# A gated recurrence with an expert layer on one core: wider transposes, evictions by PSUM bank, another order of the same operations

## The chip, the cores and the metric

The kernel runs on one core of a Trainium2 chip. The metric is the device time of one execution in microseconds. Before the change it was 181.66 us (median of 3 runs, 180.91 to 183.07). The engines are TensorE (PE, with its weight loads PEld), VectorE (DVE), ScalarE (ACT), GpSimd (POOL), and SyncE (SP), which gives out most transfers. [...]

## The reference

A recurrence runs over 768 steps for 4 sequences of 8 heads, with a state of 48 x 48 per head that decays by `w`. Its output goes through an expert layer with a maximum of two products.

```python
# r, k, v, w: (4, 8, 768, 48);  u: (8, 48);  w1, w2: (384, 1024);  w_out: (1024, 384)
for t in range(S):
    cur = einsum('bhd,bhe->bhde', u * k[t], v[t])
    y[t] = einsum('bhd,bhde->bhe', r[t], state + cur)
    state = w[t][..., None] * state + einsum('bhd,bhe->bhde', k[t], v[t])
x = y.transpose(0, 2, 1, 3).reshape(3072, 384)
out = maximum(x @ w1, x @ w2) @ w_out
```

## The kernel before

The work is cut into 12 units: 3 chunks of 256 steps for each of 4 sequences. Unit n is chunk n // 4 of sequence n % 4. A partition holds two steps that follow each other (i = 0, 1), and the 128 partitions form two blocks b of 64. The decay within a block is turned into factors on r and k (`rp`, `kp`), so that a block is a masked product of k and r, and the state passes from block to block.

The program is a list of operations, `ORDER`. The body walks through it and records each one; every engine then runs its share in that order. A name is an operation and, after the point, a unit (for weights a third of the rows). What the names do:

- loads on SyncE: `w`, `k`, `r`, `v` (384 KB each), `u`, `w1`; on GpSimd, with a cast to bf16: `w2`, `wo`; `wt` is a transposing load of w2 on SyncE
- weights: `wd` = w1 - w2 (VectorE); `wcm` = w2 x w_out (TensorE), evicted by `wce` (VectorE). With these, max(x w1, x w2) w_out = relu(x wd) w_out + x wc
- factors: `lw` = ln w (ScalarE), `lp` sum of pairs (GpSimd), `cs` running sum over the steps (TensorE, fp32), `m`, `z` (VectorE), `AO`, `AE`, `iA` exponentials (ScalarE), `rp`, `kp` products with r and k (VectorE)
- the term of u: `rk`, `rku` (GpSimd), `dg` (VectorE), `vd` (GpSimd); `vb` is v in bf16 (GpSimd)
- `tr`: transposes of r and k to PSUM; `evr` (ScalarE) and `evk` (VectorE) bring them to SBUF
- state: `kv` (TensorE), `Sa`, `Tf` (VectorE), `S1` (ScalarE), `dec`, `S0` (GpSimd); `row`, `WL` carry the last row of the factors onto partitions, `Wt` is its exponential
- `sc0`, `sc1` products of k and r (TensorE), `M0`, `M1` the masked copies (VectorE), `yb`, `yi`, `ya` the output in PSUM (TensorE), `xT` its copy (ScalarE)
- the expert layer: `g0` to `g3` (TensorE), `r0` to `r3` the relu (ScalarE), `oc`, `oa`, `ob` (TensorE), `os` the copy (ScalarE), `out` the store (SyncE, two transfers)

The parts that the change touches:

```python
@op
def tr(n):
    U[n]["tr"] = tp = pt_([P, 2, 2, 2, NP, Q], BF16, "sc")      # [128, b, j, i, p, 64]: two banks
    for j, src in enumerate((r_b, k_b)):
        for i in range(2):
            for p in range(NP):                                  # NP = 4 pairs of heads
                for e in range(2):
                    for b in range(2):
                        q = slice(b * Q, (b + 1) * Q)
                        nc.tensor.transpose(tp[e * DP:(e + 1) * DP, b, j, i, p, :],
                                            src[n % 2][q, i, 2 * p + e, :], ident[q, q])

def evict(n, j, copy):                                           # j: r or k, out of both banks
    U[n]["rk"[j] + "T"] = t = wt_([P, 2, 2, NP, Q], BF16, "rk"[j] + "T")
    copy(t.rearrange("d b i p q -> d b (i p q)"),
         U[n]["tr"][:, :, j].rearrange("d b i p q -> d b (i p q)"))

OP["evr"] = lambda n: evict(n, 0, nc.scalar.copy)
OP["evk"] = lambda n: evict(n, 1, nc.vector.tensor_copy)
...
def scores(n, i):
    rT, kT = U[n]["rT"], U[n]["kT"]
    U[n]["sc", i] = sc = pt_([P, 2, NP, P], F32, "sc")           # the same PSUM buffer as tr
    ...
                nc.tensor.matmul(sc[q, e, p, :], kT[d, b, i, p, :], rT[d, b, :, p, :])
```

Buffers: the PSUM buffers `sc` (transposes and scores), `y` and `ex` are single, `go` (expert layer) is double; the loads have three buffers each.

Of the kernel before, what the change touches and what calls it, by code (L numbers as in the profile page):

```python
# [23 lines left out]
vd.2 ob0.0 os0.0 oc1.0 oa1.0 ob1.0 os1.0 kp.2 kv.2 tr.2 Sa.2 evr.2 Tf.2 S1.2 cs.3 WL.0 Wt.0
dec.0 S0.0 g0.1 r0.1 evk.2 row.2 WL.2 Wt.2 row.1 m.3 WL.1 AO.3 z.3 AE.3 yb.2 yi.2 sc0.2 M0.2
g1.1 r1.1 g2.1 r2.1 sc1.2 M1.2 g3.1 oc0.1 oa0.1 r3.1 k.3 r.3 rk.3 rku.3 rp.3 v.3 w.4 lw.4 lp.4
vb.3 iA.3 dg.3 vd.3 ya.2 xT.2 ob0.1 os0.1 oc1.1 oa1.1 Wt.1 dec.1 S0.1 kp.3 kv.3 tr.3 Sa.3 Tf.3
evr.3 S1.3 cs.4 m.4 AO.4 z.4 AE.4 evk.3 ob1.1 os1.1 g0.2 r0.2 yb.3 yi.3 sc0.3 M0.3 out0.0 g1.2
g2.2 r1.2 r2.2 row.3 WL.3 Wt.3 sc1.3 M1.3 g3.2 r3.2 oc0.2 oa0.2 k.4 r.4 rk.4 rku.4 rp.4 v.4 w.5
lw.5 lp.5 vb.4 dg.4 vd.4 iA.4 ya.3 xT.3 ob0.2 os0.2 oc1.2 oa1.2 out1.0 kp.4 kv.4 tr.4 Sa.4 evr.4  # L30
Tf.4 S1.4 cs.5 m.5 AO.5 z.5 AE.5 evk.4 ob1.2 os1.2 g0.3 r0.3 row.4 WL.4 out1.1 yb.4 yi.4 sc0.4
M0.4 g1.3 g2.3 r1.3 r2.3 sc1.4 M1.4 g3.3 r3.3 oc0.3 oa0.3 k.5 r.5 rk.5 rku.5 rp.5 v.5 w.6 lw.6
lp.6 vb.5 iA.5 dg.5 vd.5 ya.4 xT.4 ob0.3 os0.3 oc1.3 oa1.3 out0.1 row.5 WL.5 kp.5 kv.5 tr.5 Sa.5
evr.5 Tf.5 S1.5 cs.6 m.6 AO.6 z.6 AE.6 evk.5 ob1.3 os1.3 g0.4 r0.4 yb.5 yi.5 sc0.5 M0.5 g1.4
g2.4 r1.4 r2.4 out1.2 dec.2 Wt.4 Wt.5 S0.2 sc1.5 M1.5 g3.4 r3.4 oc0.4 oa0.4 out0.2 k.6 r.6 rk.6
rku.6 rp.6 v.6 w.7 lw.7 lp.7 vb.6 dg.6 vd.6 iA.6 ya.5 xT.5 out0.3 ob0.4 os0.4 oc1.4 oa1.4 kp.6
kv.6 tr.6 Sa.6 evr.6 Tf.6 S1.6 cs.7 m.7 AO.7 z.7 AE.7 evk.6 dec.3 S0.3 ob1.4 os1.4 g0.5 r0.5
yb.6 yi.6 sc0.6 M0.6 row.6 WL.6 Wt.6 out1.3 g1.5 g2.5 r1.5 r2.5 sc1.6 M1.6 g3.5 r3.5 oc0.5 oa0.5
k.7 r.7 rk.7 rku.7 rp.7 v.7 w.8 lw.8 lp.8 vb.7 iA.7 dg.7 vd.7 ya.6 xT.6 out0.4 ob0.5 os0.5 oc1.5
oa1.5 kp.7 kv.7 tr.7 Sa.7 evr.7 Tf.7 S1.7 cs.8 m.8 AO.8 z.8 AE.8 evk.7 dec.4 S0.4 ob1.5 os1.5  # L40
g0.6 r0.6 yb.7 yi.7 sc0.7 M0.7 g1.6 g2.6 r1.6 r2.6 row.7 WL.7 Wt.7 out1.4 sc1.7 M1.7 g3.6 r3.6
oc0.6 oa0.6 k.8 r.8 rk.8 rku.8 rp.8 v.8 w.9 lw.9 lp.9 vb.8 iA.8 dg.8 vd.8 ya.7 xT.7 out0.5 ob0.6
os0.6 oc1.6 oa1.6 kp.8 kv.8 tr.8 Sa.8 evr.8 S1.8 cs.9 m.9 AO.9 z.9 AE.9 evk.8 ob1.6 os1.6 g0.7
r0.7 yb.8 yi.8 sc0.8 M0.8 dec.5 S0.5 g1.7 g2.7 r1.7 r2.7 out1.5 sc1.8 M1.8 g3.7 r3.7 oc0.7 oa0.7
k.9 r.9 rk.9 rku.9 rp.9 v.9 w.10 lw.10 lp.10 vb.9 iA.9 dg.9 vd.9 ya.8 xT.8 out0.6 ob0.7 os0.7
oc1.7 oa1.7 kp.9 tr.9 kv.9 Sa.9 evr.9 S1.9 cs.10 m.10 AO.10 z.10 AE.10 evk.9 dec.6 S0.6 ob1.7
os1.7 g0.8 r0.8 yb.9 yi.9 sc0.9 M0.9 g1.8 g2.8 r1.8 r2.8 sc1.9 M1.9 g3.8 r3.8 oc0.8 oa0.8 out1.6
k.10 r.10 rk.10 rku.10 rp.10 v.10 w.11 lw.11 lp.11 vb.10 dg.10 vd.10 iA.10 ya.9 xT.9 out0.7
ob0.8 os0.8 oc1.8 oa1.8 kp.10 kv.10 tr.10 Sa.10 evr.10 S1.10 cs.11 m.11 AO.11 z.11 AE.11 evk.10
ob1.8 os1.8 g0.9 r0.9 yb.10 yi.10 sc0.10 M0.10 dec.7 S0.7 g1.9 g2.9 r1.9 r2.9 out1.7 sc1.10  # L50
M1.10 g3.9 r3.9 oc0.9 oa0.9 k.11 r.11 rk.11 rku.11 rp.11 v.11 vb.11 iA.11 dg.11 vd.11 ya.10
xT.10 out0.8 ob0.9 os0.9 oc1.9 oa1.9 kp.11 tr.11 kv.11 Sa.11 evr.11 S1.11 evk.11 ob1.9 os1.9
g0.10 r0.10 yb.11 yi.11 sc0.11 M0.11 g1.10 g2.10 r1.10 r2.10 sc1.11 M1.11 out1.8 out1.9 g3.10
# [24 lines left out]

def _body(tc, r, k, v, w, u_in, moe_w1, moe_w2, moe_w_out, out):
    nc = tc.nc  # L80
    B, H, S, D = r.shape
# [235 lines left out]
    @op  # L317
    def tr(n):
        U[n]["tr"] = tp = pt_([P, 2, 2, 2, NP, Q], BF16, "sc")
        for j, src in enumerate((r_b, k_b)):  # L320
            for i in range(2):
                for p in range(NP):
                    for e in range(2):
                        for b in range(2):
# [1 line left out]
                            nc.tensor.transpose(tp[e * DP:(e + 1) * DP, b, j, i, p, :],  # L326
                                                src[n % 2][q, i, 2 * p + e, :], ident[q, q])

    def evict(n, j, copy):
        U[n]["rk"[j] + "T"] = t = wt_([P, 2, 2, NP, Q], BF16, "rk"[j] + "T")  # L330
        copy(t.rearrange("d b i p q -> d b (i p q)"),  # L331
             U[n]["tr"][:, :, j].rearrange("d b i p q -> d b (i p q)"))
# [49 lines left out]


    def scores(n, i):
        rT, kT = U[n]["rT"], U[n]["kT"]
        U[n]["sc", i] = sc = pt_([P, 2, NP, P], F32, "sc")
        for p in range(NP):
            for b in range(2):
                q = slice(b * Q, (b + 1) * Q)
                for e in range(2):  # L390
                    d = slice(e * DP, e * DP + D)
                    nc.tensor.matmul(sc[q, e, p, :], kT[d, b, i, p, :], rT[d, b, :, p, :])  # L392
# [156 lines left out]
```

## Time and profile before

| | |
|---|---|
| time, median of 3 | 181.66 us (180.91 to 183.07) |
| span of the profiled run (its time 180.87) | 179.0 us |
| mean granted TensorE clock | 0.986 |
| instructions in the profile | 7356 |
| VectorE, ScalarE, GpSimd busy | 99.3, 94.3, 93.7 us |
| moved by the transfers | 28.24 MB, mean 158 GB/s |

A line of a group has the source line, the engine and the operation, then output <- inputs by the program's names, the shapes and the count; after the bar the busy time in us and the mean ns of one; after the second bar the idle time of that engine just before, and what ended it. A line of the timeline has the start and the length in us, then the same names. A line of the waits has who waited for whom, the total in us, how often, and the longest. In the row of 40 slices each digit is the busy share of one slice (4.5 us here) in tenths. "issue" is a wait for nothing that the profile shows. w_sb is w2 in SBUF.

### The profile page before, as it was taken

Reading aid. Unit: us, or ns where it says so; the run is one execution under the profiler, and the core shown is the slowest. Engines: PE = TensorE matmul, PEld = TensorE weight load, DVE = VectorE, ACT = ScalarE, POOL = GpSimd, SP = SyncE. Lnnn points to the kernel's source line nnn. Section 1 sums busy time; section 2 is a strip of 40 time slices with the busy share of each in tenths; the row PEclk is TensorE's granted clock in tenths of the full one; section 3 lists DMA queues with packets and bytes.
Section 4 is the critical chain, followed back from the end, with each engine's and each line's share of the span. In section 5 each row is a group of like instructions: output and inputs, shape, how many; then the busy total and the mean of one; then the engine's idle time right before and its main releaser. Section 6 shows DMA issues by size and latency. Waiting matters only on the chain.

```text
span 179.0 us, 7356 instructions
## 1 busy us (share of the span) xinstructions
PE 137.7 (77%) x3304; PEld 91.1 (51%) x3304; DVE 99.3 (55%) x144; ACT 94.3 (53%) x165; POOL 93.7 (52%) x91
## 2 busy tenths in 40 slices
PE   0323722779968978969989899896897898999990
...
GB/s 154 202 217 304 297 108 143 296 272 85 85 290 31 182 221 44 268 139 74 198 222 163 276 57 277 147 247 178 44 278 125 80 265 14 49 4 92 64 31 87
DMA packets 63184, 28.24 MB, mean 158 GB/s; under 512 B 58152, under 2 KB 62376, under 8 KB 63152
## 3 DMA queue, kind: packets, MB, share of 16 engines
...
q0 software_dynamic: 1440, 1.57, 5.5%
q8 instruction: 26, 0.43, 0.9%
...
HBM read 23.81 MB, written 4.73 MB: 159 GB/s over the span
## 4 chain that ended last, share of the span: by engine, by line
PE 54%; issue 13%; DVE 9%; POOL 6%; ACT 4%; DMA 0%; DVEq 0%; POOLq 0%; ACTq 0%
PE go L493 14%; PE go L469 14%; PE go L488 6%; PE sc L392 5%; PE ex L237 4%; PE sc L326 4%; PE y L453 3%; DVE kT L331 3%; DVE mz L251 3%; DVE mz L247 3%; ACT ex L255 2%; PE y L346 2%; POOL rku L297 2%; PE y L432 1%; POOL rku L302 1%
## 5 line engine op out<-in xcount | busy, mean ns | idle before, releaser
L469 PE MATMUL go<-xT,wd_sb 128*128 128x256 bf16 x288 | 38.2, 277 | 1.8 <-ACT gT L477 1.8
L493 PE MATMUL go<-wo_sb,gT 128*128 128x384 bf16 x192 | 38.5, 327 | 0.0
L477 ACT ACTIVATE gT<-go 128x512 bf16<-128x512 f32 x48 | 28.5, 599 | 15.0 <-PE go L469 14.3
L396 DVE TENSOR_TENSOR M<-sc,mask 128x1024 bf16<-128x1024 f32 x24 | 29.4, 1224 | 12.5 <-PE sc L392 12.4
L469 PEld LDWEIGHTS <-wd_sb 128*128 128x128 bf16 x288 | 26.9, 99 | 9.0 <-issue 2.7
L233 POOL TENSOR_TENSOR lp<-lw 128x384 f32<-128x384 f32 x12 | 12.0, 1000 | 34.0 <-ACT lw L228 34.0
L297 POOL TENSOR_TENSOR rku<-lr,lk 128x768 f32<-128x768 f32 x12 | 21.7, 1810 | 15.3 <-issue 13.2
L493 PEld LDWEIGHTS <-gT 128*128 128x128 bf16 x192 | 17.8, 98 | 13.6 <-issue 1.8
L331 ACT COPY rT<-sc 128x1024 bf16<-128x1024 bf16 x12 | 12.1, 1012 | 20.8 <-PE sc L326 20.8
L302 POOL TENSOR_TENSOR rku<-rku,u_b 128x768 f32<-128x768 f32 x12 | 21.8, 1813 | 1.8 <-DMA u_b<-in_u_dram 1.0
L313 POOL TENSOR_TENSOR vd<-lv,dg 128x768 bf16<-128x768 f32 x12 | 17.7, 1475 | 3.9 <-DVE dg L308 3.9
L237 PE MATMUL ex<-lp,triS 128*128 128x384 f32 x24 | 13.2, 635 | 7.7 <-POOL lp L233 6.1
L228 ACT ACTIVATE lw<-lw 128x768 f32<-128x768 f32 x12 | 10.0, 837 | 13.3 <-DMA lw<-in_w_dram 13.3
L488 PE MATMUL go<-wc_sb,xT 128*128 128x384 bf16 x72 | 15.6, 326 | 0.0
L392 PE MATMUL sc<-rT,kT 48*64 48x128 bf16 x384 | 10.7, 229 | 6.3 <-DVE kT L331 5.2
L247 DVE TENSOR_TENSOR mz<-ex,lw 128x384 f32<-128x384 f32 x12 | 6.7, 557 | 14.4 <-PE ex L237 14.4
L498 ACT COPY osb<-go 128x384 f32<-128x384 f32 x24 | 11.5, 481 | 5.1 <-PE go L493 5.1
L362 DVE TENSOR_TENSOR Sa<-y,Sf 128x256 f32<-128x256 f32 x12 | 5.1, 425 | 15.3 <-PE y L346 15.3
L392 PEld LDWEIGHTS <-kT 48*64 48x64 bf16 x384 | 6.6, 110 | 11.9 <-DVE kT L331 6.8
L308 DVE TENSOR_REDUCE dg<-rku 128x16 f32<-128x768 f32 x12 | 11.4, 947 | 1.8 <-POOL rku L302 1.8
L255 ACT ACTIVATE ex<-mz 128x384 f32<-128x384 f32 x12 | 5.9, 495 | 11.8 <-DVE mz L247 7.2
L267 DVE TENSOR_TENSOR rn<-lr,ex 128x768 bf16<-128x768 f32 x12 | 11.3, 945 | 1.1 <-ACT ex L259 1.1
...
## 6 DMA issues: line engine op xcount, KB each, us to landing
lw<-in_w_dram SPq DMA_DIRECT2D x12, 384.0 KB, 6.0
lk<-in_k_dram SPq DMA_DIRECT2D x12, 384.0 KB, 3.6
lr<-in_r_dram SPq DMA_DIRECT2D x12, 384.0 KB, 4.5
lv<-in_v_dram SPq DMA_DIRECT2D x12, 384.0 KB, 5.5
...
wo_sb<-in_moe_w_out_dram POOLq DMA_DIRECT2D x1, 768.0 KB, 11.1
...
```

Source lines behind the costliest of these rows:

```text
L237: nc.tensor.matmul(EX[:, 0, 0:HD], triS, U[n]["lp"].rearrange("p h d -> p (h d)"))
L247: nc.vector.tensor_add(MZ[n % 2][:, 0, :, 0:D], ex3(), U[n]["lw"][:, :, 0, :])
L297: nc.gpsimd.tensor_mul(t, U[n]["r"], U[n]["k"])
L302: nc.gpsimd.tensor_mul(t, t, u_b.rearrange("p (h d) -> p h d", h=H).unsqueeze(1).to_broadcast([P, 2, H, D]))
L313: nc.gpsimd.tensor_mul(t.rearrange("p i h d -> p h i d"), U[n]["v"], U[n]["dg"].to_broadcast([P, H, 2, D]))
L331: copy(t.rearrange("d b i p q -> d b (i p q)"), U[n]["tr"][:, :, j].rearrange("d b i p q -> d b (i p q)"))
L392: nc.tensor.matmul(sc[q, e, p, :], kT[d, b, i, p, :], rT[d, b, :, p, :])
L396: nc.vector.tensor_mul(t.rearrange("s e p t -> s (e p) t"), U[n]["sc", i].rearrange("s e p t -> s (e p) t"), mask[:, i].rearrange("s i q - ...
L469: nc.tensor.matmul(g[:, f, :], wd_sb[:, ko, fo * P:(fo + 1) * P], U[n]["xT"][:, :, ko, :], start=(f == 0 and ko == 0), stop=(f == 1 and ko ...
L477: nc.scalar.activation(U[n]["gT"][:, 2 * j:2 * j + 2].rearrange("p f j t -> p (f j t)"), U[n]["g", j].rearrange("p f j t -> p (f j t)"), A ...
L488: nc.tensor.matmul(t, U[n]["xT"][:, b, ko, :], wc_sb[:, ko, :], start=(ko == 0), stop=False)
L493: nc.tensor.matmul(U[n]["o", b], U[n]["gT"][:, fo, b, :], wo_sb[:, fo, :], start=False, stop=(fo == FO - 1))
```

## The change

A transpose now takes two heads at once (64 rows, 128 columns), so that a unit has 32 of them and not 64. The PSUM tile has one bank for each block b. The two evictions are cut by block and no longer by r and k, so that each reads a bank of its own; this is for running ScalarE and VectorE at the same time. The readers (`scores` and the product with the state) take r and k from the tile of their block.

```diff
-                    for e in range(2):
-                        for b in range(2):
-                            q = slice(b * Q, (b + 1) * Q)
-                            nc.tensor.transpose(tp[e * DP:(e + 1) * DP, b, j, i, p, :],
-                                                src[n % 2][q, i, 2 * p + e, :], ident[q, q])
+                    for b in range(2):
+                        q = slice(b * Q, (b + 1) * Q)
+                        nc.tensor.transpose(
+                            tp[:, b, j, i, p, :],
+                            src[n % 2][q, i, 2 * p:2 * p + 2, :].rearrange("s e d -> s (e d)"),
+                            ident[q, q])
...
-    def evict(n, j, copy):
-        U[n]["rk"[j] + "T"] = t = wt_([P, 2, 2, NP, Q], BF16, "rk"[j] + "T")
-        copy(t.rearrange("d b i p q -> d b (i p q)"),
-             U[n]["tr"][:, :, j].rearrange("d b i p q -> d b (i p q)"))
+    def evict(n, b, copy):
+        U[n]["T", b] = t = wt_([P, 2, 2, NP, Q], BF16, f"T{b}")
+        copy(t.rearrange("d j i p q -> d (j i p q)"),
+             U[n]["tr"][:, b].rearrange("d j i p q -> d (j i p q)"))
-    OP["evr"] = lambda n: evict(n, 0, nc.scalar.copy)
-    OP["evk"] = lambda n: evict(n, 1, nc.vector.tensor_copy)
+    OP["ev0"] = lambda n: evict(n, 0, nc.scalar.copy)
+    OP["ev1"] = lambda n: evict(n, 1, nc.vector.tensor_copy)
...
-                    nc.tensor.matmul(sc[q, e, p, :], kT[d, b, i, p, :], rT[d, b, :, p, :])
+                    nc.tensor.matmul(sc[q, e, p, :], t[d, 1, i, p, :], t[d, 0, :, p, :])
```

The list `ORDER` is replaced as a whole by one found in another search; the operations are the same. Its beginning, and one steady stage of each (unit 5 in the recurrence, unit 4 in the expert layer):

```diff
 # the beginning
-w.0 k.0 lw.0 r.0 u wo lp.0 cs.0 m.0 z.0 AO.0 AE.0 rp.0 rk.0 rku.0 dg.0 iA.0 kp.0 tr.0 evr.0
-evk.0 v.0 vb.0 kv.0 Sa.0 Tf.0 w.1 lw.1 S1.0 k.1 vd.0 yb.0 yi.0 sc1.0 M1.0 lp.1 cs.1 m.1 AO.1
-sc0.0 M0.0 ya.0 xT.0 z.1 AE.1 w1 w2 wt.1 wcm.1 wd.2 wd.0 wd.1 wce.1 r.1 rk.1 rku.1 rp.1 v.1 vb.1
-w.2 lw.2 lp.2 iA.1 dg.1 vd.1 row.0 g0.0 g1.0 r0.0 r1.0 g2.0 r2.0 kp.1 kv.1 Sa.1 S1.1 tr.1 evr.1
-Tf.1 cs.2 m.2 AO.2 z.2 AE.2 evk.1 wt.0 wcm.0 wce.0 yb.1 yi.1 sc0.1 M0.1 wt.2 ...
+w.0 lw.0 k.0 r.0 u w2 rk.0 rku.0 dg.0 lp.0 cs.0 m.0 z.0 AO.0 AE.0 rp.0 iA.0 kp.0 v.0 vb.0 w.1 w1
+wd.0 k.1 r.1 lw.1 kv.0 Sa.0 Tf.0 S1.0 tr.0 ev0.0 ev1.0 wd.1 wo lp.1 cs.1 m.1 z.1 AO.1 AE.1 vd.0
+yb.0 yi.0 sc0.0 M0.0 sc1.0 rp.1 M1.0 iA.1 kp.1 rk.1 rku.1 dg.1 wd.2 ya.0 xT.0 tr.1 ev0.1 ev1.1
+v.1 vb.1 w.2 wt.0 wt.1 wcm.0 lw.2 wce.0 kv.1 Sa.1 S1.1 Tf.1 wcm.1 wce.1 g0.0 r0.0 vd.1 yb.1 yi.1
+sc0.1 M0.1 g1.0 g2.0 r1.0 r2.0 sc1.1 M1.1 row.0 WL.0 Wt.0 lp.2 cs.2 m.2 z.2 AO.2 AE.2 wt.2 ...
 # a steady stage
-kp.5 kv.5 tr.5 Sa.5 evr.5 Tf.5 S1.5 cs.6 m.6 AO.6 z.6 AE.6 evk.5 ob1.3 os1.3 g0.4 r0.4 yb.5 yi.5
-sc0.5 M0.5 g1.4 g2.4 r1.4 r2.4 out1.2 dec.2 Wt.4 Wt.5 S0.2 sc1.5 M1.5 g3.4 r3.4 oc0.4 oa0.4 out0.2
-k.6 r.6 rk.6 rku.6 rp.6 v.6 w.7 lw.7 lp.7 vb.6 dg.6 vd.6 iA.6 ya.5 xT.5 out0.3 ob0.4 os0.4 oc1.4 oa1.4
+tr.5 ev0.5 ev1.5 ob1.3 os1.3 out1.3 g0.4 r0.4 kv.5 Sa.5 S1.5 Tf.5 lp.6 cs.6 m.6 z.6 g1.4 r1.4 g2.4
+r2.4 vd.5 yb.5 yi.5 sc0.5 M0.5 AO.6 AE.6 rp.6 g3.4 r3.4 oc0.4 oa0.4 sc1.5 M1.5 iA.6 kp.6 rk.6
+rku.6 dg.6 v.6 w.7 lw.7 k.7 r.7 vb.6 ob0.4 oc1.4 oa1.4 os0.4 out0.4 row.5 WL.5 dec.3 S0.3 ya.5 xT.5
...
```

In the new list the loads of w, of w2 and of the next unit stand earlier, and `tr` of a unit stands before the expert layer's work of the unit before it.

More of the change, by code (lines that the diff above doesn't have):

```diff
@@ L17 @@
 ORDER = """
-w.0 k.0 lw.0 r.0 u wo lp.0 cs.0 m.0 z.0 AO.0 AE.0 rp.0 rk.0 rku.0 dg.0 iA.0 kp.0 tr.0 evr.0
-evk.0 v.0 vb.0 kv.0 Sa.0 Tf.0 w.1 lw.1 S1.0 k.1 vd.0 yb.0 yi.0 sc1.0 M1.0 lp.1 cs.1 m.1 AO.1
-sc0.0 M0.0 ya.0 xT.0 z.1 AE.1 w1 w2 wt.1 wcm.1 wd.2 wd.0 wd.1 wce.1 r.1 rk.1 rku.1 rp.1 v.1 vb.1
-w.2 lw.2 lp.2 iA.1 dg.1 vd.1 row.0 g0.0 g1.0 r0.0 r1.0 g2.0 r2.0 kp.1 kv.1 Sa.1 S1.1 tr.1 evr.1
-Tf.1 cs.2 m.2 AO.2 z.2 AE.2 evk.1 wt.0 wcm.0 wce.0 yb.1 yi.1 sc0.1 M0.1 wt.2 wcm.2 wce.2 sc1.1
-M1.1 g3.0 oc0.0 oa0.0 r3.0 k.2 r.2 rk.2 rku.2 rp.2 v.2 w.3 lw.3 lp.3 vb.2 iA.2 ya.1 xT.1 dg.2
@@ L24 @@
[L24 to L53, printed above, removed]
@@ L54 @@
-r3.10 oc0.10 oa0.10 ya.11 xT.11 out0.9 ob0.10 os0.10 oc1.10 oa1.10 ob1.10 os1.10 g0.11 r0.11
-g1.11 g2.11 r1.11 r2.11 g3.11 r3.11 oc0.11 oa0.11 out0.10 ob0.11 os0.11 oc1.11 oa1.11 ob1.11
-os1.11 out1.10 out0.11 out1.11
+w.0 lw.0 k.0 r.0 u w2 rk.0 rku.0 dg.0 lp.0 cs.0 m.0 z.0 AO.0 AE.0 rp.0 iA.0 kp.0 v.0 vb.0 w.1 w1
+wd.0 k.1 r.1 lw.1 kv.0 Sa.0 Tf.0 S1.0 tr.0 ev0.0 ev1.0 wd.1 wo lp.1 cs.1 m.1 z.1 AO.1 AE.1 vd.0
+yb.0 yi.0 sc0.0 M0.0 sc1.0 rp.1 M1.0 iA.1 kp.1 rk.1 rku.1 dg.1 wd.2 ya.0 xT.0 tr.1 ev0.1 ev1.1
@@ new lines @@
+v.1 vb.1 w.2 wt.0 wt.1 wcm.0 lw.2 wce.0 kv.1 Sa.1 S1.1 Tf.1 wcm.1 wce.1 g0.0 r0.0 vd.1 yb.1 yi.1
+sc0.1 M0.1 g1.0 g2.0 r1.0 r2.0 sc1.1 M1.1 row.0 WL.0 Wt.0 lp.2 cs.2 m.2 z.2 AO.2 AE.2 wt.2 wcm.2
+wce.2 k.2 r.2 rp.2 v.2 w.3 lw.3 vb.2 k.3 r.3 ya.1 g3.0 oc0.0 oa0.0 r3.0 xT.1 iA.2 kp.2 rk.2
+rku.2 dg.2 row.1 WL.1 ob0.0 oc1.0 oa1.0 os0.0 ob1.0 os1.0 out1.0 g0.1 r0.1 out0.0 kv.2 Sa.2 S1.2
+Tf.2 tr.2 ev0.2 ev1.2 g1.1 g2.1 r1.1 r2.1 lp.3 cs.3 m.3 z.3 vd.2 yb.2 yi.2 sc0.2 M0.2 AO.3 AE.3
+rp.3 g3.1 oc0.1 oa0.1 r3.1 sc1.2 M1.2 ob0.1 oc1.1 oa1.1 v.3 w.4 vb.3 lw.4 k.4 r.4 iA.3 kp.3
@@ new lines @@
+os0.1 out0.1 ya.2 xT.2 rk.3 rku.3 dg.3 row.2 WL.2 tr.3 ev0.3 ev1.3 Wt.1 ob1.1 os1.1 out1.1 g0.2
+r0.2 kv.3 Sa.3 S1.3 Tf.3 lp.4 cs.4 m.4 z.4 g1.2 g2.2 r1.2 r2.2 dec.0 S0.0 vd.3 yb.3 yi.3 sc0.3
+M0.3 AO.4 AE.4 rp.4 g3.2 r3.2 oc0.2 oa0.2 dec.1 S0.1 sc1.3 M1.3 iA.4 kp.4 v.4 w.5 k.5 r.5 lw.5
+row.3 WL.3 ob0.2 oc1.2 oa1.2 os0.2 out0.2 ya.3 xT.3 rk.4 rku.4 dg.4 tr.4 ev0.4 ev1.4 ob1.2 os1.2
+out1.2 g0.3 r0.3 vb.4 kv.4 Sa.4 S1.4 Tf.4 lp.5 cs.5 m.5 z.5 g1.3 r1.3 g2.3 r2.3 vd.4 yb.4 yi.4
+sc0.4 M0.4 Wt.2 dec.2 S0.2 AO.5 AE.5 rp.5 g3.3 r3.3 oc0.3 oa0.3 sc1.4 M1.4 iA.5 kp.5 v.5 w.6 k.6
@@ new lines @@
+r.6 lw.6 vb.5 rk.5 rku.5 dg.5 ob0.3 oc1.3 oa1.3 os0.3 out0.3 ya.4 xT.4 Wt.3 row.4 WL.4 tr.5
+ev0.5 ev1.5 ob1.3 os1.3 out1.3 g0.4 r0.4 kv.5 Sa.5 S1.5 Tf.5 lp.6 cs.6 m.6 z.6 g1.4 r1.4 g2.4
+r2.4 vd.5 yb.5 yi.5 sc0.5 M0.5 AO.6 AE.6 rp.6 g3.4 r3.4 oc0.4 oa0.4 sc1.5 M1.5 iA.6 kp.6 rk.6
+rku.6 dg.6 v.6 w.7 lw.7 k.7 r.7 vb.6 ob0.4 oc1.4 oa1.4 os0.4 out0.4 row.5 WL.5 dec.3 S0.3 ya.5
+xT.5 tr.6 ev0.6 ev1.6 ob1.4 os1.4 out1.4 g0.5 r0.5 kv.6 Sa.6 S1.6 Tf.6 Wt.4 lp.7 cs.7 m.7 z.7
+g1.5 g2.5 r1.5 r2.5 vd.6 yb.6 yi.6 sc0.6 M0.6 AO.7 AE.7 rp.7 g3.5 r3.5 oc0.5 oa0.5 sc1.6 M1.6
@@ new lines @@
+iA.7 kp.7 dec.4 S0.4 Wt.5 rk.7 rku.7 dg.7 v.7 vb.7 w.8 lw.8 k.8 r.8 row.6 WL.6 dec.5 S0.5 ob0.5
+oc1.5 oa1.5 os0.5 out0.5 ya.6 xT.6 tr.7 ev0.7 ev1.7 ob1.5 os1.5 out1.5 g0.6 r0.6 kv.7 Sa.7 S1.7
+Tf.7 lp.8 cs.8 m.8 z.8 g1.6 r1.6 g2.6 r2.6 vd.7 yb.7 yi.7 sc0.7 M0.7 AO.8 AE.8 rp.8 g3.6 r3.6
+oc0.6 oa0.6 sc1.7 M1.7 iA.8 kp.8 v.8 w.9 vb.8 lw.9 k.9 r.9 rk.8 rku.8 dg.8 ob0.6 oc1.6 oa1.6
+os0.6 out0.6 ya.7 xT.7 row.7 WL.7 tr.8 ev0.8 ev1.8 ob1.6 os1.6 out1.6 g0.7 r0.7 kv.8 Sa.8 S1.8
+lp.9 cs.9 m.9 z.9 g1.7 g2.7 r1.7 r2.7 vd.8 yb.8 yi.8 sc0.8 M0.8 AO.9 AE.9 rp.9 g3.7 r3.7 oc0.7
```

16 lines of the change are left out of this document (14 added, 2 removed).

## The prediction

> **What bounds the kernel now.** I read the page first (engine shares, then the 40 slices), then the waits of the DMA queue, then the timeline of one steady stretch, and last the table by stretch. A "stage" below is the time from one unit's `sc0` to the next unit's. In the timeline these starts are 43.18, 55.23, 68.27, 80.88, 91.90, 102.91, 114.41, 127.08, 139.31, 150.94 and 160.51 us for units 1 to 11.
>
> ```profile
> PE 137.7 (77%) x3304; PEld 91.1 (51%) x3304; DVE 99.3 (55%) x144; ACT 94.3 (53%) x165; POOL 93.7 (52%) x91
> PE   0323722779968978969989899896897898999990
> q8 instruction: 26, 0.43, 0.9%
> ```
>
> TensorE is the only engine near full, but only from the tenth slice on; for the first 32 us (seven slices) it is mostly idle. So there are two questions: why the front is long, and what is lost per stage. The front is in the waits of the DMA queue and of GpSimd:
>
> ```profile
> SPq L209 <- DMA w_sb<-in_moe_w_dram: 11.9, 1, 11.9
> POOL rku L297 <- issue: 13.2, 1, 13.2
> ```
>
> `w2` is given out at 18.07 us, because it stands behind `vb.0`, `vd.0` and `lp.1` in GpSimd's queue; it lands at 26.75. The transposing load `wt.1` waits for it at the head of the SyncE queue, and the load of `r.1` stands behind `wt.1`. `r.1` lands at 32.09, and only then do `rk.1`, `rp.1`, `kp.1`, `tr.1` and, at 43.18, `sc0.1` follow. The steady stage reads like this:
>
> ```profile
> 99.71 1.01 ACT L331 COPY rT<-sc 128x1024 bf16<-128x1024 bf16 x1 [1.54 <-PE sc L326]
> 100.53 0.56 DVE L247 TENSOR_TENSOR mz<-ex,lw 128x384 f32<-128x384 f32 x1 [0.49 <-PE ex L237]
> 101.12 0.49 ACT L255 ACTIVATE ex<-mz 128x384 f32<-128x384 f32 x1
> 101.70 0.56 DVE L251 TENSOR_TENSOR mz<-ex,lp 128x384 f32<-128x384 f32 x1 [0.62 <-ACT ex L255]
> 102.18 0.68 DVE L331 COPY kT<-sc 128x1024 bf16<-128x1024 bf16 x1
> 102.91 0.24 PE L392 MATMUL sc<-rT,kT 48*64 48x128 bf16 x1 [0.59 <-DVE kT L331]
> 77.20 0.41 PE L326 MATMUL sc<-ident,kn 64*64 64x64 bf16 x28 [1.44 <-issue]
> ```
>
> The eviction `evk` is ready for VectorE at 100.72 but stands behind `m` and `z`, and `z` waits for `AO`. So `sc0` waits for kT, 0.6 to 1.1 us per stage. The last line is another loss: TensorE stops in the middle of the transposes for nothing that the profile shows. Such stops of 1.56, 0.96, 1.44, 1.62 and 1.06 us stand at 51, 64, 76, 122 and 135 us, always in the kv and transpose stretch. The stretches show both:
>
> ```profile
> 91.90:103.40 11.50, 10.67 (x288) 7.21 (x289) 7.70 (x10) 8.30 (x17) 8.82 (x9) 1.00 0.76 192
> 114.40:127.00 12.60, 10.47 (x268) 7.07 (x268) 7.24 (x9) 7.64 (x15) 9.04 (x8) 1.00 0.59 159
> ```
>
> (Columns: window, length, then busy time of TensorE, weight loads, VectorE, ScalarE, GpSimd, granted clock, DMA share, GB/s.) TensorE's work is about the same in both, the length is not.
>
> [...] Before, both evictions read both banks, and the trace agrees that they take turns: unit 0's kT starts at 14.85, when rT (13.81 + 1.01) has ended. After, each reads one bank. But in the built program every `ev1` on VectorE still waits for the count that `ev0` on ScalarE raises. So I expect no overlap: they still run one after the other. [...] transposes of about 200 ns start some 10 ns apart. [...] The trace has 26 instruction packets in 0.43 MB, 16.5 KB each. [...] `wo`, given out by GpSimd at 3.2 us, took 11.1 us, and `v.0`, given out at 4.14 by SyncE, landed at 14.9.
>
> **The transposes.** 64 per unit with 64x64 tiles become 32 with 64x128. Before, a unit's 64 start within 0.66 us (110.41 to 111.07), 10 ns each. The closest thing to the new tile is `yb`, with stationary tiles of the same shape:
>
> ```profile
> L414 PE MATMUL y<-ident,vd 64*128 64x64 bf16 x144 | 4.3, 195 | 1.1 <-DVE Tf L371 1.1
> L326 PE MATMUL sc<-ident,rn 64*64 64x64 bf16 x384 | 5.8, 201 | 3.3 <-DVE rn L267 3.3
> ```
>
> Its 12 take 0.28 us (101.73 to 102.01), 23 ns each; 32 x 23 = 0.75 us. So TensorE gains nothing here: 0.1 us per unit is lost, 1 us in all. What it gains is 768 instructions fewer of some 6,600 and a thinner stretch where the stops are. The evictions keep their shape (128x1024), about 1.01 and 0.68 us, 1.7 in sequence.
>
> **The steady stage after.** TensorE's steps, by differences of starts from 102.9 to 114.4: two `sc` 0.70, `g0` 0.75, `g1`+`g2` 1.41, `g3` 0.67, two `oc` 0.97, `oa` and `ob` 2.81, `ya` 0.84, `kv` 0.27, `cs` 0.75, `yb` 0.28, `yi` 0.30, transposes 0.66: 10.4; with the new transposes 10.5. The new order puts `tr` at the start of the stage and `sc0` some 5 us later, with `ob1`, `g0`, `kv`, `cs`, `g1`, `g2`, `yb`, `yi` between. From the end of `ya` at 0: `xT` 0.1 to 0.9, `ev0` to 2.0, `ev1` to 2.75, while `sc0` is due at 5.3. The eviction is hidden even in sequence. `M0` then ends at 7.0, `rp` 7.95, `M1` 9.2, `kp` 10.2, and the next `tr` is due at 10.5. The first of the two stretches above has 7.7 us of VectorE, 8.3 of ScalarE and 8.8 of GpSimd in a stage, so TensorE is the bound at 10.5, barely.
>
> A second loop is as long. The SyncE queue holds, in turn, `out0`, `row`, `WL`, `out1`, `v`, `w`; and ScalarE takes `lw` of that same `w` ahead of `os0` and `xT`:
>
> ```profile
> 93.31 1.11 SPq L504 DMA_DIRECT2D out_dram<-osb  x2
> 102.29 0.26 SPq L277 DMA_DIRECT2D row<-mz  x1
> 103.86 0.38 SPq L282 DMA_DIRECT2D WL<-row  x1
> lr<-in_r_dram SPq DMA_DIRECT2D x12, 384.0 KB, 4.5
> lw<-in_w_dram SPq DMA_DIRECT2D x12, 384.0 KB, 6.0
> ```
>
> `out0` 1.11, `row` to `WL` 1.57, `WL` 0.38, `out1` 1.11, `v` 0.6, landing of `w`, now second of four as `r` is before, 4.5, `lw` 0.84, `os0` 0.48: 10.6, with six hand-overs about 11.0. I take 10.9 per stage, where before had (160.51 - 43.18)/10 = 11.73.
>
> **The front after.** `w2` goes out at about 3.3 us, where `wo` did[...]; `w1` now stands before `k.1` and `r.1`. Before, everything up to `w.1` (five loads of 0.39 MB, `u`, `wo`: 3.7 MB) had landed at 16.1 us. `w1` adds 1.57 MB; at the 300 GB/s of slices 4 and 5 that is 5.2 us: 21.3. VectorE has `wd.0` ahead of `Sa.0` and `ev1.0`, so unit 0 stops there. With the mean durations of the groups: `wd.0` to 22.5, `Sa.0`, `Tf.0`, `ev1.0` to 24.1, `wd.1`, `m.1`, `z.1` to 26.4, `M0.0` 27.6, `rp.1` 28.6, `M1.0` 29.9, `kp.1` 30.9, `dg.1` 31.8, `wd.2` 33.0. TensorE: `tr.1` 31.7, `wcm.0` 33.0, `kv.1` 33.3, `wcm.1` 34.6, `g0.0` 35.4, `sc0.1` at 36.2 (before 43.18). Up to `sc0.2` come 13.7 us of TensorE work, 1.3 of them `wcm.2`: 50 (before 55.23). By then `g1.1` and `g2.1` are done, which before came after `sc0`.
>
> **Sum.** 50 + 9 x 10.9 = 148.1; the last stage has no `cs`, -1.0 (before 9.57 against 11); from `sc0.11` to the end before 160.51 to 179.0 = 18.5, less the 1.4 of `g1.10` and `g2.10`: 17.1. Span 164.2; the time lay 1.9 above the span (180.87 and 179.0): 166.
>
> **Rivals.** (a) The SyncE loop binds: `w` lands late, `lw` holds `os0` and `xT`, TensorE waits for `xT` before `g0`. For it: the median landing of `w` of 6.0. Then about 11.8 per stage and 175 us. Against: there `w` was last of four. (b) The stops in TensorE's stream go on, 0.5 us per stage on average, or only move: 170. (c) The front is not shortened, since `w1` before `r.1` holds VectorE at `wd.0`: 6 us lost, 172. (d) Evictions overlap after all: nothing gained, they are off the path. (e) Stages at TensorE's 10.5 and `sc0.2` at 46: 158.
>
> **Range and chances.** A stage error of 0.5 us is 4.5 us, the front is good to 5; together 158 to 175. To miss 2% (178 us) both the front gain and the stage gain would have to fail. Faster 0.89, same 0.08, slower 0.03.
>
> **What would show it.** Right: `ev1` starts only after `ev0` ends; `sc0` no longer waits for an eviction; 32 transposes take 0.7 to 0.8 us; `wt.0` no longer waits 11.9 us; `sc0.1` near 36; stages of 10.5 to 11.2. Wrong: ScalarE waiting for `lw` in steady stages with TensorE waiting for `xT`; stops of over 1 us in the kv stretch; `wd.0` later than 23 us.

## The result and the profile after

| | before | after |
|---|---|---|
| time, median of 4 runs, us | 182.28 (180.91 to 183.07) | 171.91 (171.86 to 172.66) |
| span of the profiled run, us | 179.0 | 170.9 |
| `sc0.1`, `sc0.2`, `sc0.11` start at, us | 43.18, 55.23, 160.51 | 37.18, 50.76, 153.31 |
| stages from `sc0.2` to `sc0.11`, mean | 11.70 | 11.39 |
| from `sc0.11` to the end, us | 18.5 | 17.6 |

The ratio of the times is 0.945, 95% interval 0.938 to 0.952. Of the 8.1 us between the two spans, 6.0 are gained before `sc0.1`; the stage to `sc0.2` gives 1.5 back (13.58 us, before 12.05); the nine stages to `sc0.11` bring 2.7, and the end 0.9. (The profiled runs of e2, e6 and e11 below were over 1% slower than other runs of the same kernel: from them only the stops and single starts are used, and the times given are those of the other runs.)

The page of the changed kernel: engine shares, TensorE's 40 slices, the instruction queue.

```profile
PE 136.6 (80%) x2920; PEld 90.0 (53%) x2920; DVE 98.6 (58%) x144; ACT 94.1 (55%) x165; POOL 96.0 (56%) x91
...
PE   0003273999999599999799995997989999989990
...
q8 instruction: 23, 0.38, 0.9%
```

TensorE is full from the eighth slice (slices of 4.3 us), two earlier than before, and 384 matmuls and three instruction packets are gone (with their weight loads 768 instructions, 256 for each packet). But the row still has dips: 5, 7, 5, 5, 7. The waits say who is behind them:

```profile
ACT lw L228 <- DMA lw<-in_w_dram: 15.2, 8, 3.0
DVE T L332 <- ACT T L332: 13.3, 7, 3.8
PE go L470 <- ACT xT L462: 3.2, 5, 1.8
```

The first line: ScalarE waits eight times for `w`. Before, it did so three times, 9.8 us of it at once in the front:

```profile
ACT lw L228 <- DMA lw<-in_w_dram: 13.3, 3, 9.8
```

The third line of the changed kernel follows from its first, on TensorE. The second says that VectorE's eviction still comes after ScalarE's. The stretches of the changed kernel, cut at `sc0` (columns as in the prediction), show that stages are of two kinds:

```profile
50.76:64.69 13.93, 11.96 (x245) 7.66 (x237) 8.33 (x12) 7.72 (x14) 9.90 (x10) 0.88 0.70 169
64.69:75.03 10.34, 10.34 (x251) 7.02 (x244) 7.46 (x10) 7.62 (x14) 5.68 (x5) 1.00 0.71 179
...
86.50:96.90 10.40, 10.40 (x266) 7.07 (x253) 7.44 (x10) 7.70 (x15) 7.94 (x10) 1.00 0.70 175
96.90:109.20 12.30, 10.51 (x262) 7.05 (x252) 7.41 (x10) 7.68 (x15) 7.51 (x7) 1.00 0.72 173
```

Where length and TensorE's busy time are the same (10.34, 10.40), TensorE is the bound. In the last stretch its work is the same and 1.8 us are lost. The timeline of that stage:

```profile
96.16 2.14 SPq L505 DMA_DIRECT2D out_dram<-osb  x2
...
98.98 0.67 SPq L179 DMA_DIRECT2D lw<-in_w_dram  x1
...
103.46 0.84 ACT L228 ACTIVATE lw<-lw 128x768 f32<-128x768 f32 x1 [3.04 <-DMA lw<-in_w_dram]
104.21 0.46 ACT L499 COPY osb<-go 128x384 f32<-128x384 f32 x1
104.57 0.80 ACT L462 CAST xT<-y 128x768 bf16<-128x768 f32 x1
...
105.42 0.81 PE L470 MATMUL go<-xT,wd_sb 128*128 128x256 bf16 x6 [1.79 <-ACT xT L462]
```

Read it from below. TensorE waits 1.79 us for `xT`; `xT` stands behind `os0` and `lw` on ScalarE, whose 164 instructions of the list start in the list's order; `lw` waits 3.04 us for `w`; and `w` was given out only at 98.98, because the stores `out0` (at 92.26) and `out1` (at 96.16, 2.14 us of SyncE) stand before `v` and `w` in SyncE's queue, and each store waits for ScalarE's copies, as SyncE's own waits say:

```profile
SPq L505 <- ACT osb L499: 36.9, 12, 6.6
```

Read so, a late `w` makes late stores, and these make the next `w` late.

### The profile page after: what moved, and what is told of

It reads as the page before. It is cut to its first block, busy times and chain, and to the rows that moved or that the text cites. A ratio compares the mean times of both kernels' runs of the same rounds, so it can differ in the third digit from the quotient of the medians.

```text
span 170.9 us, 6596 instructions
## 1 busy us (share of the span) xinstructions
PE 136.6 (80%) x2920; PEld 90.0 (53%) x2920; DVE 98.6 (58%) x144; ACT 94.1 (55%) x165; POOL 96.0 (56%) x91
## 4 chain that ended last, share of the span: by engine, by line
PE 30%; DMA 26%; ACT 12%; POOL 9%; DVE 8%; SPq 7%; issue 5%; ACTq 0%; POOLq 0%; DVEq 0%
DMA lw<-in_w_dram 15%; PE go L470 8%; PE go L494 7%; DMA u_b<-in_u_dram 4%; SPq L505 4%; PE go L217 3%; PE go L489 3%; POOL rku L302 3%; ACT T L332 3%; SPq L179 3%; DMA lv<-in_v_dram 3%; ACT xT L462 3%; DMA lk<-in_k_dram 3%; PE ex L237 2%; POOL rku L297 2%
## 5 line engine op out<-in xcount | busy, mean ns | idle before, releaser
L494 PE MATMUL go<-wo_sb,gT 128*128 128x384 bf16 x192 | 39.2, 331 | 0.0
L292 POOL CAST vn<-lv 128x768 bf16<-128x768 f32 x12 | 9.9, 826 | 26.9 <-DMA lv<-in_v_dram 20.1
L237 PE MATMUL ex<-lp,triS 128*128 128x384 f32 x24 | 12.3, 599 | 14.2 <-POOL lp L233 14.2
L494 PEld LDWEIGHTS <-gT 128*128 128x128 bf16 x192 | 17.3, 98 | 11.5 <-issue 0.3
L313 POOL TENSOR_TENSOR vd<-lv,dg 128x768 bf16<-128x768 f32 x12 | 19.6, 1633 | 4.5 <-DVE dg L308 4.3
L228 ACT ACTIVATE lw<-lw 128x768 f32<-128x768 f32 x12 | 10.1, 840 | 15.2 <-DMA lw<-in_w_dram 15.2
L332 DVE COPY T<-sc 128x1024 bf16<-128x1024 bf16 x12 | 8.3, 689 | 13.4 <-ACT T L332 13.3
L263 ACT ACTIVATE ex<-mz 128x768 f32<-128x768 f32 x12 | 9.8, 816 | 8.8 <-DVE rn L267 8.8
L271 DVE TENSOR_TENSOR kn<-lk,ex 128x768 bf16<-128x768 f32 x12 | 11.4, 946 | 5.3 <-ACT ex L263 5.3
L332 ACT COPY T<-sc 128x1024 bf16<-128x1024 bf16 x12 | 12.2, 1017 | 0.7 <-PE sc L325 0.6
## 6 DMA issues: line engine op xcount, KB each, us to landing
wo_sb<-in_moe_w_out_dram POOLq DMA_DIRECT2D x1, 768.0 KB, 10.6
```

Of the source, the lines that this page charges most:

```text
L237: nc.tensor.matmul(EX[:, 0, 0:HD], triS, U[n]["lp"].rearrange("p h d -> p (h d)"))
L313: nc.gpsimd.tensor_mul(t.rearrange("p i h d -> p h i d"), U[n]["v"], U[n]["dg"].to_broadcast([P, H, 2, D]))
L332: copy(t.rearrange("d j i p q -> d (j i p q)"), U[n]["tr"][:, b].rearrange("d j i p q -> d (j i p q)"))
L494: nc.tensor.matmul(U[n]["o", b], U[n]["gT"][:, fo, b, :], wo_sb[:, fo, :], start=False, stop=(fo == FO - 1))
```

## The experiments

Two questions: which part of the change brought the gain, and what holds the stages above TensorE's 10.4 us. The theory at the start was the prediction's: the order brings it, and the transposes bring nothing of their own. The rival: TensorE's stops vanish because of the transposes' fewer instructions. For the stages: the loop through SyncE and ScalarE, against the landing of `w` alone. In the runs of these experiments the kernel before took 178.1 to 182.0 us, so ratios count, each against runs of before on the same chip.

| kernel | ratio (95%) | the seven stages from `sc0.3` to `sc0.10`, us | `sc0.2`, us |
|---|---|---|---|
| before | 1 | 11.01 to 12.67 | 55.2 |
| e1: new transposes, old order | 0.970 (0.961 to 0.980) | 11.25 to 11.29 | 52.3 |
| e2: old transposes, new order | 0.982 (0.971 to 0.993) | not used | 50.9 |
| the change | 0.945 (0.938 to 0.952) | 10.34 to 12.32 | 50.8 |
| e7: the change, `out1` behind the loads | 0.912 (0.904 to 0.920) | 10.34 to 10.98 | 50.9 |

**e1, the transposes alone.**

```diff
 # the changed kernel's code, with the ORDER of before and only the names changed
-... tr.5 Sa.5 evr.5 Tf.5 ... evk.5 ...
+... tr.5 Sa.5 ev0.5 Tf.5 ... ev1.5 ...
```

> The order of before, with only the new transposes (64x128) and the evictions by bank. Theory A (the gain is all in the order): 181 to 184 us, the same within 1%, since the transposes take as long on TensorE as before (0.7 to 0.8 us per unit) and the second eviction still starts after the first. Rival B (the transposes bring a part: 768 fewer instructions, no more stops of TensorE in the kv and transpose stretch): the stops of 1.0 to 1.6 us, 6.6 us in all, go, and the time is 175 to 178 us.

Measured 173.75 us, ratio 0.970: more than half of the whole gain without any new order. In its profile TensorE has not one stop marked "issue", where before had 7.3 us of them, and its seven stages are even, 11.25 to 11.29 us. In place of the wait for kT it has another (who waits, total, count, longest):

```profile
PE y L431 <- DVE T L330: 7.5, 9, 0.8
...
DVE T L330 <- ACT T L330: 2.7, 3, 1.7
```

Evicted by block, both tiles are needed by `yi`, which stands ahead of `sc0`. So these stages are longer than before's shortest of 11.0, but none of the seven is 12 to 13. The theory that the order brings everything falls.

**e2, the order alone.**

```diff
 # the kernel before's code, with the new ORDER and only the names changed
-tr.5 ev0.5 ev1.5 ob1.3 os1.3 out1.3 ...
+tr.5 evr.5 evk.5 ob1.3 os1.3 out1.3 ...
```

> The order of after, with the old transposes (64x64) and the evictions by r and k. Theory A: 171 to 173 us, as the changed kernel. Rival B: the stops come back in the kv and transpose stretch, and the time is 175 to 179 us. If the evictions by bank mattered for the wait of sc0, sc0 would wait for the second eviction again; theory A expects none, as sc0 stands some 5 us later.

Measured 176.48 us, ratio 0.982. The front is that of the changed kernel (`sc0.1` 37.3, `sc0.2` 50.9), so the whole gain of the front is the order's. It is also all that the order gains alone: 1.8% are 3.3 us, and its `sc0.2` comes 4.3 us sooner than before's. Five stops of TensorE are back, at other places than before:

```profile
72.42 0.70 PE L467 MATMUL go<-xT,wd_sb 128*128 128x256 bf16 x5 [0.68 <-issue]
82.96 0.38 PE L324 MATMUL sc<-ident,kn 64*64 64x64 bf16 x23 [0.97 <-issue]
93.80 0.35 PE L324 MATMUL sc<-ident,rn 64*64 64x64 bf16 x20 [0.43 <-issue]
121.24 0.28 PE L344 MATMUL y<-vn,kn 64*64 64x64 bf16 x7 [1.02 <-issue]
133.42 0.68 PE L467 MATMUL go<-xT,wd_sb 128*128 128x256 bf16 x3 [1.35 <-issue]
```

The two parts together, 3.0% and 1.8%, make about the 5.5% of the change, within the intervals.

**e5, each transpose twice.** Is it the new tile, or the number of instructions? With each transpose given out twice, the old order has as many instructions as before, with the new tile. (The second writes the same values again.)

```diff
+                        for _ in range(2):
-                        nc.tensor.transpose(
+                            nc.tensor.transpose(
                             tp[:, b, j, i, p, :], ...
```

> The order of before with the new transposes, but each transpose given out twice (the second writes the same values again): TensorE has as many instructions as before in the same places, 64 per unit in the transposes, now with the wide tile. Theory F (the stops of TensorE come with the instruction stream, not with the shape of the tile): stops of 1.0 to 1.9 us come back at the places of before, in the kv and transpose stretch of five or six units, some 7 us in all, and with 32 more transposes of 23 ns per unit (0.75 us, 9 us in all) the time is 187 to 192 us. Theory G (the 64x64 tiles cause the stops): no stops, 181 to 184 us.

Measured 185.46 us, ratio 1.024 (1.011 to 1.038), slower than before, though not by as much as theory F expected; the stops are 4.4 us and not 7. Against e1, 5.4% or about 10 us are lost: these 4.4, and twelve times the 0.47 us by which a stage without stops grew (11.75 against 11.28). The evictions by bank are the same in e1 and e5, so they are not what removed the stops. The stops are back, after the same instruction as before (the count at the start of the group: before's stops stood ahead of the last 6, 15 and 28 transposes):

```profile
54.57 0.29 PE L324 MATMUL sc<-ident,kn 64*128 64x64 bf16 x6 [0.85 <-issue]
66.52 0.41 PE L324 MATMUL sc<-ident,kn 64*128 64x64 bf16 x15 [0.83 <-issue]
79.25 0.59 PE L324 MATMUL sc<-ident,kn 64*128 64x64 bf16 x28 [1.04 <-issue]
```

So the stops go with the position in the instruction stream, and neither with the tile nor with the time. There is a counterpart in the instruction queue. Cutting its view into windows of 0.1 us gives the moment of each instruction packet:

| kernel | packet at, us | TensorE goes on at, us | between |
|---|---|---|---|
| before | 50.62 / 62.47 / 74.77 / 121.55 / 133.35 / 144.85 | 53.05 / 64.69 / 77.20 / 123.75 / 135.66 / 147.27 | 2.4 / 2.2 / 2.4 / 2.2 / 2.3 / 2.4 |
| e5 | 52.15 / 64.05 / 76.85 | 54.57 / 66.52 / 79.25 | 2.4 / 2.5 / 2.4 |
| e3 (its first stop) | 46.55 | 48.91 | 2.4 |
| the change (its only stop, 0.88 us) | 81.35 | 83.69 | 2.3 |
| e11 (below) | 56.75 / 67.75 / 111.65 / 123.15 | 59.42 / 70.09 / 114.09 / 125.43 | 2.7 / 2.3 / 2.4 / 2.3 |

In all 15 cases TensorE goes on 2.2 to 2.7 us after a packet. In the traces of before and of the changed kernel each of these packets has 16,384 bytes (the 16.5 KB of the prediction are 0.43 MB over 26), and there are three fewer for 768 instructions fewer (26 and 23). The places of the stops go by 256 instructions, too. Count in before's trace what TensorE has begun when it stops (weight loads, matmuls and its few instructions that only wait): at the six stops of the table these are 1217, 1729, 2241, 4545, 5057 and 5569, and each is 256 n + 193, where n (4, 6, 8, 17, 19 and 21) is the number of packets until then. The only other stop of over 0.2 us in before (0.24 us, at 103.39) stands at 3521, with n = 13, and that of the changed kernel at 2497, with n = 9. Packets without a stop lie between (in before at 54.3, 66.1 and 78.6): there TensorE came to the place 6.2 to 6.4 us after the packet.

So a stop goes with an instruction packet. That TensorE waits there for the packet fits all of this, but no row of the trace shows it. In these two traces the 256 instructions ahead of a stop took 2.9 to 4.2 us, all others (the front's included) 6.5 in the median; four of those took 2.9 to 3.5 without a stop, and there TensorE came to the place 2.3 to 3.6 us after the packet. What sets the moment of a packet is not shown. In the order of before, the kv and transpose stretch is where instructions are shortest: 96 matmuls and as many weight loads before, the matmuls started within 0.93 us where nothing stops (87.63 to 88.56); 64 in e1.

**e3, the new place of w2 alone.**

```diff
-w.0 k.0 lw.0 r.0 u wo lp.0 ... AE.1 w1 w2 wt.1 ...
+w.0 k.0 lw.0 r.0 u w2 lp.0 ... AE.1 w1 wo wt.1 ...
```

> The kernel before with one swap in the order: w2 is given out where wo was and wo where w2 was. Nothing else. If the front of before is long because wt.1 waits for w2 in the SyncE queue ahead of r.1, sc0.1 moves from 43 us to about 35 and the time falls by 5 to 7 us, to 175 to 177. Rival: the bandwidth binds (the same bytes must land before the expert layer can start), sc0.1 moves by under 3 us, and the time is 179 to 182.

Measured 178.1 us, ratio 0.985 (0.982 to 0.988). `sc0.1` starts at 38.8, so 4.4 of the 6.0 us of the front come from this exchange, less than the 8 that were expected: `wcm` here waits 4.4 us for `wo`. The time, too, fell by less than was expected. And the stops stand at the same instructions although all is some 4 us earlier, and have not become shorter (8.4 us for six): 

```profile
48.91 0.25 PE L324 MATMUL sc<-ident,kn 64*64 64x64 bf16 x6 [1.79 <-issue]
60.64 0.32 PE L324 MATMUL sc<-ident,kn 64*64 64x64 bf16 x15 [1.04 <-issue]
73.16 0.41 PE L324 MATMUL sc<-ident,kn 64*64 64x64 bf16 x28 [1.45 <-issue]
```

**e6, evictions at once.** Each bank a PSUM tile of its own, so that `ev1` waits for TensorE alone. (The masked copies, which read the same buffers, are cut in halves for it.)

```diff
-U[n]["tr"] = tp = pt_([P, 2, 2, 2, NP, Q], BF16, "sc")
+U[n]["tr"] = tp = [pt_([P, 2, 2, NP, Q], BF16, f"s{b}") for b in range(2)]
```

> The changed kernel with one PSUM tile for each bank, so that the second eviction waits for TensorE and no longer for the first; the masked copies are cut in two halves for that, one per bank. The evictions start within 0.1 us of each other in the steady stages where VectorE is free. Theory (evictions are off the path in this order): the time stays within 1% of the changed kernel, 171 to 174 us, perhaps 0.5 us more for the twelve times two extra instructions of VectorE. Rival (the serial eviction costs its 0.7 to 1.0 us per unit): 162 to 166 us.

Now `ev1` does not wait for `ev0`: in unit 0 both start at 21.6 us, and later VectorE's can come first (once at 104.53 against 107.37). The time is 171.83 us, ratio 0.947 (0.938 to 0.956): that of the change. The overlap for which the evictions were cut is worth nothing here, since they are off the path.

**e4, lw later.** Is it enough that ScalarE takes `lw` after `xT`, so that a late `w` does not hold it?

```diff
-... v.6 w.7 lw.7 k.7 r.7 vb.6 ... ya.5 xT.5
+... v.6 w.7 k.7 r.7 vb.6 ... ya.5 xT.5 lw.7     # and so for units 4 to 11
```

> The changed kernel with lw of the units from 4 on given to ScalarE after xT instead of before os0 and xT. Theory C (the steady stages lost 0.5 us against the forecast because ScalarE waits for the load of w ahead of os0 and xT): the waits of ScalarE for w no longer hold xT, TensorE's waits for xT (3.2 us in 5) go, the stage of unit 3 no longer has its 2 us stop before the transposes of k, and the time is 165 to 169 us. Rival D (the loads themselves and GpSimd bind, the wait only moves to lp and cs): 170 to 173 us, with waits of TensorE for cs or for vd in place.

Measured 170.38 us, ratio 0.949 (0.938 to 0.960), not told apart from the change: the rival's range. TensorE's wait for `xT` falls from 3.2 to 0.5 us, but `lp` (GpSimd) and with it `cs` come later. In the waits, 14.0 of the first line belong to the front:

```profile
PE ex L235 <- POOL lp L231: 18.1, 7, 14.0
...
POOL vn L290 <- DMA lv<-in_v_dram: 16.6, 6, 5.1
```

The second line says that GpSimd, too, waits for a late load, that of `v`: that points to the queue of the loads, and not to ScalarE's order alone.

**e7, the stores behind the loads.** The other end of the loop: `out1` (and `out0.0`) no longer stand before the loads of their stage.

```diff
-tr.5 ev0.5 ev1.5 ob1.3 os1.3 out1.3 g0.4 ... v.6 w.7 lw.7 k.7 r.7 vb.6 ...
+tr.5 ev0.5 ev1.5 ob1.3 os1.3 g0.4 ... v.6 w.7 lw.7 k.7 r.7 out1.3 vb.6 ...
```

> The changed kernel with the second store of a unit (out1) given out after the loads of the stage instead of before them. Theory H (the loop through the SyncE queue binds the steady stages: the loads stand behind a store that waits for ScalarE's copy, and ScalarE's lw stands ahead of that copy): the loads go out some 2 to 3 us sooner, ScalarE no longer waits for w nor GpSimd for v, the stages of units 2 to 10 come to 10.5 to 10.9 us from 11.4, and the time is 165 to 169 us. Rival (the bandwidth or GpSimd's own work binds): 170 to 172 us.

Measured 164.91 us (164.67 to 165.56), ratio 0.912 (0.904 to 0.920): faster than both kernels. Its page and its stretches:

```profile
PE 135.2 (83%) x2920; PEld 89.8 (55%) x2920; DVE 98.9 (61%) x144; ACT 94.0 (58%) x165; POOL 95.9 (59%) x91
...
PE   0004184899999999999999999999999999989990
```

```profile
50.90:61.20 10.30, 10.30 (x244) 7.00 (x236) 8.09 (x12) 7.37 (x14) 8.65 (x10) 1.00 0.32 70
...
92.90:103.30 10.40, 10.40 (x268) 7.07 (x252) 7.46 (x10) 7.83 (x15) 7.45 (x7) 1.00 0.73 180
```

The dips are gone, and from `sc0.2` on all stages but one are 10.3 to 10.6 us. In the timeline, in the same place as the one above, `w` is given out at 90.87, 2.1 us before `sc0.6` (92.94), where the change gave it out 2.1 us after it (98.98 and 96.90). The long store (3.08 us of SyncE) stands behind the loads, where it holds none of them, and `lw` does not wait here:

```profile
90.87 0.57 SPq L177 DMA_DIRECT2D lw<-in_w_dram  x1
...
92.62 1.14 SPq L177 DMA_DIRECT2D lr<-in_r_dram  x1
...
93.85 3.08 SPq L503 DMA_DIRECT2D out_dram<-osb  x2
...
96.49 0.85 ACT L226 ACTIVATE lw<-lw 128x768 f32<-128x768 f32 x1
```

In the whole run, ScalarE's waits for `w` fall from 15.2 us to this:

```profile
ACT lw L226 <- DMA lw<-in_w_dram: 4.0, 3, 2.2
```

GpSimd still waits for `v`, 14.2 us in six (20.1 in seven in the change), which theory H did not expect; the stages run near TensorE's bound all the same. So the place of the stores ahead of the loads is shown as the cause of the lost time. That lateness went round in a loop is read from the timeline and not shown by itself: e4, which cut the loop at `lw` and left the stores in their place, only moved the wait.

**e8, e9, e10, more on top of e7.** e8 adds e4's edit and a change of the front, which takes GpSimd's `rk.0`, `rku.0` behind `kp.0` (they wait there for `u`, before `lp.0`) and `wd.0`, `wd.1` out of the way of unit 0. e9 has the front edit alone, e10 that of e4 alone.

```diff
-... u w2 rk.0 rku.0 dg.0 lp.0 ... kp.0 v.0 ... wd.0 k.1 ... wd.1 wo ...        # e8, e9
+... u w2 lp.0 ... kp.0 rk.0 rku.0 dg.0 v.0 ... k.1 ... wo ... wd.0 wd.1 wd.2 ...
-... w.7 lw.7 k.7 ... xT.5 ...                                                # e8, e10
+... w.7 k.7 ... xT.5 lw.7 ...
```

> The changed kernel with lw after xT, out1 after the loads, and the front reordered (rk.0, rku.0, dg.0 after kp.0, so that lp.0 doesn't stand behind u; wd.0 and wd.1 next to wd.2, so that unit 0 doesn't wait for w1). By theories C and H stages of 10.5 us; unit 0 is 5 us earlier, but kp.1 waits for the load of r.1 at 25.7 us, so that the front gains 1 to 2 us: 163 to 166 us. Rival (the front gains nothing, as the loads of k.1 and r.1 and the transposing loads hold it): 166 to 169 us.

> The kernel of e7 (stores out1 behind the loads of their stage) with the front of e8 alone: rk.0, rku.0, dg.0 behind kp.0, and wd.0, wd.1 beside wd.2. It parts the two edits that e8 added to e7. If it was lw behind xT that cost e8 its 6 us (lp and cs late, stages of 10.9), this runs at 163 to 166 us with stages of 10.4, and sc0.1 is no earlier than 37. If it was the front edit (M and wc_sb late in the first two stages, an order that stays behind), it comes near 168 to 171 us.

> The kernel of e7 with the other edit of e8 alone: from unit 4 on, lw stands right behind xT of two units before. If lw behind xT is the loss, stages are 10.8 to 11.0, TensorE waits for lp before cs, and the time is 168 to 171 us. If it is not, stages stay at 10.4 and the time at 164 to 166.

Measured: e8 171.03 us, ratio 0.943 (0.934 to 0.952); e9 168.14, 0.941 (0.932 to 0.949); e10 167.95, 0.938 (0.932 to 0.944). All three lose against e7 (0.912), and e8 lies outside both ranges that were expected. Each part loses by itself and in a way of its own, but the two losses, of about 3% each, do not add up in e8. In e10 the seven stages are 10.8 to 10.9 where e7 has 10.4, with this in the waits (13.2 of the second line are the front's, as in e7):

```profile
POOL lp L231 <- ACT lw L226: 27.0, 9, 4.7
...
PE ex L235 <- POOL lp L231: 16.3, 8, 13.2
```

In e9 the stages are e7's, but `sc0.2` starts at 54.1 and not 50.9. Unit 0 does come sooner (`sc0.0` at 18.8, in e7 at 24.6), but the work put off fills the stages behind it; `ya` waits once 6.2 us for the masked copy of VectorE. So bringing unit 0 forward in this way gains nothing.

**e11, the old transposes in e7's order.**

```diff
 # the kernel before's code, with the ORDER of e7 and only the names changed
-tr.5 ev0.5 ev1.5 ob1.3 os1.3 g0.4 ...
+tr.5 evr.5 evk.5 ob1.3 os1.3 g0.4 ...
```

> The order of e7 with the transposes and evictions of before (64 of 64x64, evr and evk over both banks). It asks what the new transposes are worth once the wait for w is gone. If the stops of TensorE for nothing that the profile shows come with the longer instruction stream, as e1, e2 and e5 say, four or five of them of about 1 us come back and the time is 168 to 170 us against 164.9. If in this order they hide in waits, as part of them may have in e2, it is within 1 us of e7.

Measured 166.64 and 167.57 us, ratio 0.933 (0.923 to 0.944), against e7's 0.912 (0.904 to 0.920), between the two outcomes that were expected. Four stops are back, 3.8 us in all, of which one:

```profile
125.43 0.49 PE L467 MATMUL go<-xT,wd_sb 128*128 128x256 bf16 x3 [1.32 <-issue]
```

So in this order the new transposes are worth about 2%; e11's side of it rests on two runs.

## Why the prediction was right and where it was wrong

The time, 171.91, lies in the range of 158 to 175, and 5.9 us above the 166 that was named. By its own steps:

- **The front: right.** `sc0.1` was put at 36.2 and came at 37.18; `sc0.2` at 50 and came at 50.76. The cause, `w2` given out behind GpSimd's work and `wt.1` behind it, is shown by e3 for 4.4 us of it. `wd.0` ran at 20.21 (put at 21.3), and VectorE did hold unit 0 up.
- **The transposes: the cost right, their worth wrong.** The 32 were put at 0.75 us; they take 0.58 (starts from 102.23 to 102.81 in the changed kernel). But "TensorE gains nothing here" let the saved instructions stand as an aside: the sum held no term for the stops, and rival (b) took 0.5 us per stage for their going on. e1 shows that the thinner stretch by itself is worth 3.0% of the time, with every stop gone.
- **Evictions: right.** `ev1` waits for `ev0` (13.3 us in seven waits), `sc0` waits for no eviction, and overlapping them brings nothing (e6), as rival (d) put it. Only the wait of before was read too long: `sc0` waited for kT 5.2 us in nine, 0.6 the longest, and not 0.6 to 1.1 in each stage.
- **TensorE's bound of a stage: right.** Put at 10.5; 10.34 and 10.40 where nothing else holds it, and 10.3 to 10.6 in all but one stage of e7.
- **The step that failed: 9 x 10.9 - 1.0 = 97.1 us.** Measured 153.31 - 50.76 = 102.55. The loop through SyncE was seen, as "a second loop", and rival (a) named its signs; but it was taken as an even 10.9 that binds in no stage by more than 0.4. Of the 5.45 us, 3.0 lie in the stage from `sc0.2` (13.93). There TensorE waits 1.97 us for `kp.3`, as `lw.4`, waiting 2.87 us for its load, stands before `iA.3` and so before `kp.3`; and its work takes 11.96 us for 245 matmuls (e7: 10.30 for 244), as the granted clock is halved for 3.4 us, from 58.3 to 61.7. So about half of what this stage lost is the clock and not the loop. Then 1.7 lie in the next seven (11.14 on average, from 10.34 to 12.32); and 0.75 in the last, which was not 1.0 shorter (10.65). Terms of the loop that were too small: the landing of `w`, 4.5 in the sum, has a median of 5.1, and a store's 1.11 was 1.74 to 2.14 in the slow stages. With 5.1 the same sum gives 11.2, without hand-overs.
- **The gain of the stages: put down to the wrong part.** The prediction gave it to the order and to hidden evictions. e2 has both with the old tiles, and gains no more than its front; e1 has neither and evens out its stages. It takes the new transposes for the stops to go and, in e7, the new place of the stores for the rest.
- **The end: right within 0.5.** Put at 17.1, came at 17.6.

So the sum missed to one side, by 0.8 us at `sc0.2`, 5.45 in the stages and 0.5 at the end, and the range took it in. That it could do without a term for the stops was luck: the new transposes took away all but 0.9 us of them, which the prediction had named but not counted. e7, with the loads first and one stop of 0.4 us, runs at 164.9, near the 166. Not settled is why the granted clock fell in the stage from 50.76. It fell at 58.27, at the end of a wait of TensorE of 1.97 us (to 58.44), but whether for that reason wasn't tried; and the profiled run was the slowest of its four (172.66, the others 171.86 to 171.94), so they may lack it.
